# Low words of the weights and first key copies on GpSimd instead of ScalarE, with all steps in another order of issue

## The chip, the core and the metric

The kernel runs on one core of one Trainium2 chip. The metric is device time in microseconds (us). Five engines work side by side, each through its own instructions in order: TensorE (matmuls, PE in the profile, its weight loads PEld), VectorE (DVE), ScalarE (ACT), GpSimd (POOL) and SyncE (SP), which here issues every transfer (DMA). An instruction waits on semaphores for what it needs, and while it waits everything behind it on the same engine waits too.

## What is computed

A gated delta-rule attention over 4 batches of 8 heads, 768 tokens of 48 features, and behind it an MLP mixer over tokens and channels. Cut to what matters:

```python
k_n = k / (np.linalg.norm(k, axis=-1, keepdims=True) + 1e-06)
for t in range(S):
    y[:, :, t] = q_t @ state                     # per batch and head
    state = state + beta_t * outer(k_t, v_t - k_t @ state)
x = y as (B, S, H*D)
h = np.maximum(x.transpose(0, 2, 1) @ w_tok1, 0.0) @ w_tok2
u = x + h.transpose(0, 2, 1)
return u + np.maximum(u @ w_ch1, 0.0) @ w_ch2    # float32
```

q, k, v and beta come as float32. The four weight matrices come as float64 (768x256, 256x768, 384x1536, 1536x384), and the kernel turns them into float32 on the chip.

## The kernel before

**Units and steps.** The sequence is cut into 24 units of 128 tokens of one batch (all 8 heads of it). The recurrence over tokens is done in 36 steps: r0 to r23 take 64 tokens of batches 0 and 1, r24 to r35 take 64 tokens of batches 2 and 3 together. Before a unit can be walked, its triangular 64x64 blocks have to be inverted; units are inverted in rounds (i0 takes units 0 to 3, i1 takes 4 and 5, later ones up to four).

**Jobs.** Every part of the work is a Python generator whose `yield`s cut it into steps. For a unit u: `k` loads keys and queries (`load_kq`, L406), `v` loads and scales values (L449), `p` makes norms, masks and turned copies (`prep`, L528), `c` and `d` make the products of keys with keys and queries (`grams`, L504), `t` hands the diagonal blocks to the inversion (`to_parts`, L668), `h`, `f` and `j` put the inverse together. `i` is the inversion of a round (L717), `r` a recurrence step (`recur`, L903; `recur_pair`, L983), `m` the mixer of batches 0 and 1 (L1586), and `T`, `A`, `F`, `B` that of batches 2 and 3. `w0` to `w33` each turn one piece of a weight matrix into float32 (`round_weights`, L271). `x`, `z` and `Y` issue matmuls on zeros.

**The order.** One long string (L1775 to L1845) lists 2610 steps; a loop takes them one after the other and calls `next` on the job named. So the string alone sets the order of instructions on every engine and of transfers on the sync queue. Semaphores and buffers are put in by the framework; assertions in the jobs say what must have been issued before.

**A weight piece** (128 rows, 384 or 256 columns) has four steps. Step 0 loads it as 64-bit words into one of three landing buffers `d64` (L280); a fourth piece can only be loaded when the first one's buffer has been read for the last time. Step 1 is two ScalarE instructions, one on the high words of the float64s (L286) and one on the low words (L287), both in place and with a stride of two words. Step 2 shifts the high words on VectorE (L289). Step 3 adds the two on GpSimd as integers into the resident weight (L293), and frees the landing buffer.

**Keys of the first units.** Units 0 to 3 have their keys stacked from the padded copy that is on the chip already, by four copies of 64 partitions each (L435, on ScalarE); half of these copies go from one half of the partitions to the other. Later units load the stacked form from memory (`stacked`, L440). Step 0 of `p` (L539) squares the stacked keys on ScalarE.

**Into the first inversion.** `t0` to `t3` each have a ScalarE copy (L674), a VectorE copy (L677) and a GpSimd copy (L679), and i0 begins with a VectorE transpose of what the four have written (L731). The inversion then runs on VectorE in pairs of small instructions (L739, L744).

**A recurrence step** is a chain: matmuls (L920), a VectorE subtraction (L927), matmuls (L940, L944), a ScalarE copy (L950), matmuls (L958, L959), a VectorE update of the state (L967) and two ScalarE copies of the output (L972).

Of the kernel before, what the change touches and what calls it, by code (L numbers as in the profile page):

```python
# [23 lines left out]
def kernel(  # L24
# [102 lines left out]
    for par in range(2):  # L127
        for n0, n1, first in ((0, (B - 1) * NP, par), ((B - 1) * NP, B * NP, 1 - par)):
            nc.gpsimd.tensor_copy(
                out=pick[:, par, n0:n1],  # L130
                in_=ident[: B * H, 2 * n0 + first : 2 * n1 : 2],
# [139 lines left out]
    def round_weights(dst, src, name):  # L271

        n = dst.shape[-1]
        d64 = loads.tile([128, WP], mybir.dt.int64, name="d64", bufs=3)[:, 0:n]
        nc.sync.dma_start(out=d64, in_=src)  # L280
# [5 lines left out]
        nc.scalar.activation(a, a, ACTF.Prelu, scale=2.0**-112, alpha=2.0**32)  # L286
        nc.scalar.activation(lo, lo, ACTF.Copy, scale=2.0**-29)  # L287
        yield
        nc.vector.tensor_scalar(  # L289
            out=f, in0=hi, scalar1=3, scalar2=None, op0=ALU.logical_shift_left,  # L290
        )
        yield
        nc.gpsimd.tensor_tensor(out=dst.bitcast(U32), in0=f, in1=lo, op=ALU.add)  # L293
# [112 lines left out]
    def load_kq(u):  # L406
# [25 lines left out]
        heads = kpad[slot(u)].rearrange("t (p par) d -> t p par d", par=2)  # L432
        for cc in range(2 if u < RU else 0):
            for par in range(2):
                nc.scalar.copy(kst[PAR[par ^ cc], :, cc], heads[PAR[cc], :, par, 0:D])  # L435
# [1346 lines left out]
    h0 h1 h0 w8*2 h1 Y i0 f0 Y p4 f1 h2*2 p5*3 f0*2 w6 h0*5 k6*5 p6 z f2*2 k8*3 p5
    w6 p5 p3 p5 j0*3 f1*2 h1*5 j0*2 w8*2 w17 f2 h2*3 v0 t4*2 w17 r0*5 p6 h2*2 c5*2
    v1 w11*2 j1 p5 k7*2 c5 k7 c5 r0 c5 r0*2 w14*2 v1 w11*2 k7*2 p7 d5*5 r1*5 w14*2
    p6*2 t5 j1 t5*2 r1*2 j1 j2 p7 h3*2 r1*3 p6*3 i1*2 r2*5 k8*2 f3*2 w9 k9*3 j1*2
    v2*2 i1*3 j2*2 r2*2 f3 i1*2 p6*3 w16 v2 w16*3 r2*2 h3 r2 i1 d6 r3*5 i1*2 w9*3
    v2 d6 h3 v2 w0 h3*2 r3 h3 d6*2 w0 d6 j3 c6*5 r3*4 w0 j2 w0 p8*2 j2 r4 p8 r4*4
# [8 lines left out]
    i2*2 r10*4 w12 i2 k12 i2*2 m0 w32 k11 k12 w32 r10*2 m0 p11 k12*4 w19 p11 r10  # L1796
    c10 r10 c10 r10 w33 d10*2 q2 Y r11*4 v7 r11*3 w19 c10 q1 w30 c10 r11 k12*2
    i2*3 r11 v6*4 i2*5 m0*3 i2*5 q5 i2 m0 p11*4 c10 p11 m0 p11*2 m0*2 k12*2 w12
    m0*3 v6 f6*3 w12 d11 c11*2 d11*2 c11 w33 c11 d11*2 j6 p12 w12 m0 w33 w30*3
    p12*2 f7*3 j6*2 m0 c11 j7 f6 f8 w27*2 f8 j7 f8 w15 f7 m0 w29 w33 w29 j7 r12*4  # L1800
    w31 j8 p11 t10*3 r12 Y r12 f9 j8 f9 w21 p12 r12 f8 r13*2 w15*2 r12 w15 r13*3
    w31*3 Y r13*2 w33 j8 w21 m0 r13 q4 p12*4 r13*2 m0*2 r14 c12 f9 j9 r14*2 w21
    t10 w20*2 v7 r14*2 c12*2 w33 c12 r14 v8 c12*2 r14*2 w25*2 j9 r14 r15 v8 w21
    r14 r15 w25 r15*3 w25 k13*4 w20 k13*4 p13 k13*2 w20 v8*3 m0*2 p13 w25 p13 m0
    r15 p13 r15 p13 w27 w25 k13*2 j9 m0*4 p13 f9 w23 t12*3 p13 t12 w25 r15*3 c13*6
    w23 k14*7 r16*5 m0 p13 m0*3 w23*4 k14 r16*2 t11 t13*2 j9*2 t11*3 w33 p14 r16*2
    p14*2 w31 m0*3 w31 m0 w31 m0 w23 r17*2 r16 t13 r17 t13 r17*2 p14*2 m0*2 p14 i3
    k14*4 i3*3 k15 v9*2 m0*3 v10 i3*5 k15 i3 r17 k15*2 p14 k15*3 m0 v10*2 i3 k15*2
    m0*2 k15*2 i3*4 r17*4 k15 i3*2 p14 m0*2 i3*6 m0*4 r18 i3 r18*2 v9*3 r18*2 i3*8
    m0*10 v10*2 m0 r18 c14*4 r18*2 m0*2 f10 c14 f10*2 f12*2 p15*3 m0*4 r18 r19 r18  # L1810
    r19*3 j10 f10 j10*2 f12 p15 f11*4 f12 r19 c14 r19 v11 p15*3 k16*7 j11 m0*2
    r19*4 j11 j12 r20*3 k16*2 r20 m0 r20 k16*3 v11 m0 j11 r20*2 v11*2 p15 c15*2
    p10 r20*2 c15 r20 c15*3 f13*3 p16 r21*5 m0 r21*2 p16*4 k17*7 p16 j12*2 p16 k17
    r21*3 m0*3 r22 c16 r22*3 k17*4 v11 r22 c16*4 r22*2 m0 r22 t14 p17 f13 c16 t14
    j13*2 t14 r22 r23 t15*2 t16 r23*2 r22 r23 m0*3 r23 t15*2 r23 p17*5 t16 p17 j13
    t16*2 m0*3 t14 c17*5 r23*2 c17 t17*2 m0*8 p17 t17*2 i4*3 v12 m0 k18 v15*2 i4
    m0 i4 m0 i4*3 m0 i4 k18*2 j13 p16 m0*2 j13 i4*4 m0 v12*3 k18*4 v12 k18 r24*2
    r23 v13*5 m0 k18*4 v15*2 i4*2 m0*2 p18 i4 p18 r24*3 m0 r24 i4 m0 p18*2 r25*4
    p18 k19*8 i4 m1 r25 i4 m1*4 i4 m1 v14 i4*2 v14 i4*8 r24*3 r25*2 m1 v14 i4*2
    v14*2 p18*2 r25 m1*2 p19 m1*5 k19*4 p19 f14*2 r25*5 c18*5 f14 c18 p18 r26*3  # L1820
    p19*2 j14 p19*3 r26*2 f15*4 f14 m1*2 j14 m1 j14 j15*3 s*2 f17*2 m1 f17 m1
    f16*3 p19 f16 k20*8 j16*3 j17 m1 r26*3 p20 m1*2 p20 r26*2 c19*2 r26 c19 v15
# [60 lines left out]
```

## Time and profile before

| | us |
|---|---|
| median of 3 runs | 625.72 |
| the runs | 620.05, 625.72, 627.02 |
| span of the profiled execution | 619.7 |
| TensorE busy in it | 590.3 (95%) |
| VectorE busy | 469.1 (76%) |
| ScalarE busy | 256.9 (41%) |
| GpSimd busy | 109.9 (18%) |
| moved by DMA | 55.52 MB, mean 90 GB/s |

The profiled execution's own time is its span, 619.7 us; it lies 0.4 us under the fastest run and 6.0 under the median. A row of a group reads: line, engine, operation, output<-inputs, shapes, count, then busy time in us and mean ns of one, then the idle time of the engine just ahead of these instructions and what ended it. A row of the timeline reads: start in us, duration in us, engine, line, operation, and in brackets the idle time ahead and what ended it. Ends of matmuls are modelled, so a busy TensorE isn't TensorE at its peak.

### The profile page before, as it was taken

Reading aid. Unit: us, or ns where it says so; the run is one execution under the profiler, and the core shown is the slowest. Engines: PE = TensorE matmul, PEld = TensorE weight load, DVE = VectorE, ACT = ScalarE, POOL = GpSimd, SP = SyncE. Lnnn points to the kernel's source line nnn. Section 1 sums busy time; section 2 is a strip of 40 time slices with the busy share of each in tenths; the row PEclk is TensorE's granted clock in tenths of the full one; section 3 lists DMA queues with packets and bytes.
Section 4 is the critical chain, followed back from the end, with each engine's and each line's share of the span. In section 5 each row is a group of like instructions: output and inputs, shape, how many; then the busy total and the mean of one; then the engine's idle time right before and its main releaser. Section 6 shows DMA issues by size and latency. Waiting matters only on the chain.

```text
span 619.7 us, 20909 instructions
## 1 busy us (share of the span) xinstructions
PE 590.3 (95%) x8733; PEld 515.9 (83%) x8733; DVE 469.1 (76%) x1160; ACT 256.9 (41%) x682; POOL 109.9 (18%) x150
## 2 busy tenths in 40 slices
PE   8588997999999999999999999999999999999998
PEld 5467875667898988877889888897699999999997
DVE  5987875986889855697566996866888898685874
ACT  8758796448521344223551215415352331414200
POOL 2348264225311122003020120010000000000000
PEclk9878797999999999999999999999999999999999
DMA  9667567667653254454445443135102012020001
GB/s 219 136 135 169 138 142 185 129 155 179 126 114 72 67 116 83 95 113 99 92 87 126 83 95 83 32 66 140 32 2 39 1 21 47 12 52 13 14 26 51
DMA packets 154605, 55.52 MB, mean 90 GB/s; under 512 B 129648, under 2 KB 148976, under 8 KB 154512
## 3 DMA queue, kind: packets, MB, share of 16 engines
q1 hardware_dynamic: 154512, 54.20, 39.1%
q8 instruction: 68, 1.11, 0.8%
q14 instruction: 25, 0.20, 0.1%
HBM read 41.19 MB, written 11.21 MB: 85 GB/s over the span
## 4 chain that ended last, share of the span: by engine, by line
PE 74%; DVE 9%; DMA 4%; ACT 4%; issue 2%; SPq 1%; POOL 1%; DVEq 0%; POOLq 0%; ACTq 0%
PE p_c L1668 13%; PE p_r L1498 13%; PE p_o L1689 10%; PE p_a L1570 7%; PE p_b L1570 6%; PE p_g L511 3%; DMA d<-in_moe_w_ch_dram 3%; PE p_h L1608 3%; DVE sub L739 2%; PE p L1593 2%; DVE x L744 2%; PE p_k L920 2%; PE p L1223 1%; PE p_h L1238 1%; PE p_y L1034 1%
## 5 line engine op out<-in xcount | busy, mean ns | idle before, releaser
L1668 PE MATMUL p_c<-u_t,wc 128*128 128x256 f32 x432 | 101.6, 386 | 0.5 <-issue 0.5
L1668 PEld LDWEIGHTS p_c<-u_t,wc 128*128 128x128 f32 x432 | 79.6, 190 | 11.9 <-issue 1.1
L1689 PE MATMUL p_o<-wc,r 128*128 128x192 f32 x360 | 64.6, 331 | 0.7 <-DVE xb L1628 0.7
L739 DVE TENSOR_TENSOR sub<-x 128x84 f32<-128x84 f32 (+24 forms) x178 | 58.4, 328 | 7.4 <-DMA x<-n_dram 2.8
L744 DVE TENSOR_TENSOR x<-x,sub 128x84 f32<-128x84 f32 (+24 forms) x178 | 58.2, 327 | 6.1
L1689 PEld LDWEIGHTS p_o<-wc,r 128*128 128x128 f32 x360 | 58.4, 190 | 2.3 <-DVE xb L1628 1.3
L1677 ACT ACTIVATE r<-p_c 128x512 f32<-128x512 f32 x36 | 21.4, 596 | 51.2 <-PE p_c L1668 46.1
L511 PE MATMUL p_g<-kq 48*64 48x128 f32 (+1 forms) x704 | 34.9, 283 | 4.0 <-ACT kq L587 3.3
L517 DVE TENSOR_TENSOR gm<-p_g,mb 128x512 f32<-128x512 f32 x44 | 28.9, 683 | 8.1 <-PE p_g L511 7.5
L484 POOL TENSOR_TENSOR v_st<-v_st,nrm 128x384 f32<-128x384 f32 x12 | 10.3, 856 | 131.9 <-DMA v_st<-in_v_dram 104.4
L574 POOL TENSOR_TENSOR mb<-mask_c,cs 128x512 f32<-128x512 f32 x20 | 21.2, 1062 | 67.8 <-DVE cs L552 36.9
L511 PEld LDWEIGHTS p_g<-kq 48*64 48x64 f32 (+1 forms) x704 | 26.5, 137 | 7.6 <-ACT kq L587 4.3
L293 POOL TENSOR_TENSOR wc<-w_f,d 128x384 uint32<-128x384 uint32 x24 | 24.6, 1029 | 42.8 <-ACT d L287 14.1
L1511 DVE TENSOR_TENSOR kq<-kq,p_r 128x384 f32<-128x384 f32 x40 | 21.0, 551 | 10.7 <-PE p_r L1498 8.8
L1498 PE MATMUL p_r<-t_d,wc 128*128 128x192 f32 x160 | 28.8, 326 | 0.0
L1511 DVE TENSOR_TENSOR gm<-gm,p_r 128x384 f32<-128x384 f32 x40 | 21.1, 551 | 8.1 <-PE p_r L1498 5.8
L400 DVE STREAM_TRANSPOSE kq<-pads 128x512 f32<-128x512 f32 x24 | 25.5, 1108 | 2.0 <-PE p_w L1038 1.6
L1498 PEld LDWEIGHTS p_r<-t_d,wc 128*128 128x128 f32 x160 | 26.5, 190 | 0.0
L1689 PE MATMUL p_o<-wc,s 128*128 128x192 f32 x144 | 25.7, 330 | 0.6 <-DVE xb L1628 0.6
L1498 PE MATMUL p_r<-pads,wc 128*128 128x192 f32 x128 | 25.4, 326 | 0.0
L1628 DVE TENSOR_TENSOR xb<-xb,p_o 128x192 f32<-128x192 f32 x42 | 14.6, 348 | 13.0 <-PE p_o L1689 12.6
L1689 PEld LDWEIGHTS p_o<-wc,s 128*128 128x128 f32 x144 | 23.3, 190 | 1.2 <-DVE xb L1628 0.9
(315 smaller groups left out, 1387.1 us busy)
## 6 DMA issues: line engine op xcount, KB each, us to landing
d<-in_moe_w_ch_dram SPq DMA_DIRECT2D x24, 384.0 KB, 4.2
v_st<-in_v_dram SPq DMA_DIRECT2D x96, 48.0 KB, 2.9
out_dram<-xb SPq DMA_DIRECT2D x23, 192.0 KB, 2.1
kst<-in_k_dram SPq DMA_DIRECT2D x64, 48.0 KB, 2.8
n_dram<-gm SPq DMA_DIRECT2D x72, 32.0 KB, 2.3
pads<-in_k_dram SPq DMA_DIRECT2D x24, 96.0 KB, 2.9
...
```

What stands on the lines that cost most here:

```text
L293: nc.gpsimd.tensor_tensor(out=dst.bitcast(U32), in0=f, in1=lo, op=ALU.add)
L400: nc.vector.transpose(kq_of[p // 2][:, i, :, p % 2].rearrange("f p (s g) -> f p g s", g=G), rows_of[i].rearrange("s p (g d) -> s p g d", g ...
L511: nc.tensor.matmul(p_g[PAR[i ^ cc ^ swap(u)], p], kqt[f, p, cc, 0], kqt[f, p, cc])
L517: nc.vector.tensor_tensor(out=blocks(gm_of(u))[:, :, cc, D:GW].rearrange("s p (two n) -> s p two n", two=2), in0=p_g, in1=made[u][:, :, cc ...
L739: nc.vector.tensor_tensor(out=tmp, in0=y[:, :, 0:s, s : s + 1].to_broadcast([n, k, s, w]), in1=y[:, :, s : s + 1, s + 1 : m].to_broadcast( ...
L744: nc.vector.tensor_tensor(out=y[:, :, 0:s, s + 1 : m], in0=y[:, :, 0:s, s + 1 : m], in1=tmp, op=ALU.add,)
L1498: nc.tensor.matmul(p[:, i], pieces[q // width][:, at : at + 128], f[f"u{n}"], start=first and i == 0, stop=True, skip_group_check=True,)
L1511: nc.vector.tensor_tensor(out=o, in0=o, in1=p, op=op_of(sign))
L1570: nc.tensor.matmul(p, a[:, i], w[:, i // 2, i % 2], start=first and i == 0, stop=True, skip_group_check=True,)
L1668: nc.tensor.matmul(p_c[:, k], piece_of(wc1, cb, f * 128)[:, f * 128 : (f + 1) * 128], u_t[:, cb], start=(cb == 0), stop=(cb == NCB - 1),)
L1677: nc.scalar.activation(r2[:, m], p_c, ACTF.Relu)
L1689: nc.tensor.matmul(p, a[:, m], wc2[:, m, j], start=(start and i == 0), stop=(i == NM - 1), skip_group_check=True,)
```

## The change

Two instructions change their engine, and the order string is another one. The jobs, the transfers, the buffers and the number of steps of each job stay as they are (2610 steps, the same count for every job, the `x`, `z` and `Y` among them).

```diff
         nc.scalar.activation(a, a, ACTF.Prelu, scale=2.0**-112, alpha=2.0**32)
-        nc.scalar.activation(lo, lo, ACTF.Copy, scale=2.0**-29)
+        nc.gpsimd.tensor_scalar(out=lo, in0=lo, scalar1=2.0**-29, scalar2=None, op0=ALU.mult)
...
-                nc.scalar.copy(kst[PAR[par ^ cc], :, cc], heads[PAR[cc], :, par, 0:D])
+                nc.gpsimd.tensor_copy(out=kst[PAR[par ^ cc], :, cc], in_=heads[PAR[cc], :, par, 0:D])
```

The first is issued 34 times (28 of 128x384 words, 6 of 128x256), the second 16 times (64 partitions, 4 runs of 48 words). The string, in its first lines before and after:

```diff
-    w10 x*4 z w10*2 z w1*4 k1*3 z k1*3 z b p1 z p1 k0*6 p0*2 b*2 p1 w2 p0*5 p1*2
-    w10 p0*2 z w3 w2 c0*3 p0 w3*2 d0*2 w3 c0 p1 c0 d0*3 k2*3 v1 p1*2 w18 k2*2 p1*2
-    c1*2 d1 k2 p2*2 c1 t0 d1 c1*2 d1*3 t0 p2*8 c2*2 w2 d2 c2*3 Y d2 w2 k3*6 p3
-    d2*2 p3 d2 t1*3 x p3*7 c3 k4*5 k7 w13 w18*2 d3*2 v1*2 v0*2 c3*3 v0 c3 d3*3 t0
...
+    w10 x*2 w10*2 w1 x*2 w1 k1 Y k1*4 z k1 b w1 k0*2 w1 k0*4 z*4 p1*2 w3 b*2
+    p0*10 k2*2 k3 k2 k3 w2 p1*2 w10 w3 k3 p1 z c0 k2 d0 c0*2 k2*2 p2 w3 p2 c0
+    d0*2 c0 p2 k3 d0*2 p1*5 k3 w18 x w3 t0 c1 k3 c1*3 d1 c1 d1 p2 d1*3 t0 k4 k5
+    k4*3 w2 p2*5 x*2 c2*3 p2 c2*2 d2*2 w13 p3*2 t1 w13 w18 w2 w18 w2 d2 p3 d2*2
+    p3*2 t0 t1 k4 p3*3 k5 p3 d3*3 k5 d3 w18 d3 c3*5 t2 t1 p4*2 k5*2 t3 t2*2 k6 t3
```

And around the recurrence steps r8 to r11 (the whole string is reordered in this manner, each job's own steps in their sequence):

```diff
-    w27*2 w7*2 d9*4 c9*2 f5 c9*3 t7*2 t8 r7*2 t7*2 j4*2 v4 p10*2 h5 r8*3 w29 t8*3
-    w29 w27*2 r8*2 w29*2 q3 w29 j4*2 r8 w22*4 t9*3 r8*3 p9 r9 p10 r9*3 t9 v5 h5*3
-    j5 i2 r9 w4*2 r8 h5 i2*5 w4 i2 w19*2 k10 w32 p10*2 w32 v7 k12 m0*2 k11 k12 q0
-    v5*3 p10*2 r9*2 j5*2 k11*3 i2*2 r9 w4 i2 j5 i2*3 p10 v5 r9*2 d10*3 r10 v7*2 j5
...
+    w7 w22 d9*3 f5 d9 f5 p9 c9*5 t9*2 r7 t9*2 v4 r8*3 w29 j4*2 h5 k11 i2 w27 j4
+    w27 j4 h5 r8*2 w27 Y*2 w29 r8*2 p10*3 r8*2 w29 r9*2 w4 r9 w22 r9*2 r8 h5*2 r9
+    w22 j5 p10*2 v6 r9 i2 w19 h5 i2 p10*2 r9 i2*2 q2 r9 i2 d10 w4*2 i2 p10 m0
+    i2*2 k11 v5*2 w22 j5 d10 j5 i2*2 r10*4 i2*2 v5*3 w32 w19*2 k11 r9 i2 k11 p11
+    k11 r10 j5 i2 w4 w19 m0 i2 m0 p11 j5 r10 w12 w30 m0 k12*3 r10*2 i2*2 d10 p11
```

The weight pieces come in nearly the same sequence in both (w10, w1, then w2 and w3 in turn, w18, w13, w17, and so on).

More of the change, by code (lines that the diff above doesn't have):

```diff
@@ L1782 @@
[L1782 to L1787, printed above, removed]
@@ L1795 @@
-    v5*3 p10*2 r9*2 j5*2 k11*3 i2*2 r9 w4 i2 j5 i2*3 p10 v5 r9*2 d10*3 r10 v7*2 j5
[L1796 to L1822, printed above, removed]
@@ new lines @@
+    p4*2 t3 i0*5 w13 i0*3 k7 i0*3 p5 i0*2 p4*2 w13 v0 k5 k6 v0 p4 w17 i0*2 k4
+    p4*2 d4*2 c4 d4*2 v1 c4*2 w8 v0*2 w6 w8 p4 w6 i0 c4*2 w17 d4 Y*2 k8 z k6 z p5
+    z*2 v1*2 w6 k6 v1 h0*2 t4 k6 p5 h1*2 v1 i0 w6 f0 f1 f0 k6 f1 p5*2 h2 p5 f0 h0
+    x h0 p3 h0*2 f1 h0 w14 p5 k7 p5 h2 w8*2 f2*3 j0*2 p6 j0 p5 t4 h1*4 k7 j1 k7
+    w11 h1 j0*2 v0 w14 k7 h2*4 c5 h2 w14*2 w0 r0 w17 r0*3 c5*3 d5*2 p6 r0*2 p6
+    d5*2 t4 c5 r0 p5 r0 p7 r1*3 p6 r1*2 w11 j1 d5 k8 t5 r1 p7 r1 h3*2 r1 p6 j1
+    w11 p6 t5 j2 f3*2 r1 r2*2 w17 r2*2 j1*2 v2 t5 i1 r2 j2 p6 r1 v2 j2 r2 i1*6 f3
@@ new lines @@
+    r7*2 d8 h4*2 w27 d8 t8*4 h4*2 r7*2 h4 t7 p10 p9*3 p8 p9 r7 j4 r7 p9 d9 q3 f5
+    w7 w22 d9*3 f5 d9 f5 p9 c9*5 t9*2 r7 t9*2 v4 r8*3 w29 j4*2 h5 k11 i2 w27 j4
[3 more added lines that the diff above has]
+    k11 r10 j5 i2 w4 w19 m0 i2 m0 p11 j5 r10 w12 w30 m0 k12*3 r10*2 i2*2 d10 p11
+    c10*2 r10 w32 k12*3 w32 d10 c10*2 r11 k12 r11*2 k12*2 r11 d10 r11 Y r10 r11
@@ new lines @@
+    q0 v7 r11 i2 w12 r11*2 p11 i2 w12 v6 i2 m0 i2 w32 k12 i2 k12*2 w12 i2 q5 p12
+    m0 v7 v6 w33 w15 i2*6 v6 p11 m0 i2*2 p11 v7*2 m0 c10 p11*3 m0*3 f6 m0 f6*2
+    w33 m0*2 f7*2 d11 f7 f6 f9 c11 p11 f8 f9*2 f7 c11*4 f8*2 w15*3 w30*2 j6 d11*3
+    w30 w33 d11 t11 m0 j6*2 t11 f9 w33 m0 f8 j7 w33 j7 w33 m0 j7 w25 p12 v6 r12*4
+    p12*2 r12*2 j8*2 r12 r13*3 r12 w27*2 v7 s j9 j8 r13 w21 m0 r13 w31 q4 p12 k13
+    w25 k13*7 p12 r13 p12 m0 r13*2 p12 c12*2 r13 k13 w31*3 r14*2 w20 q1 r14*2 r13
+    c12*2 r14 v8 c12*2 r14 w25 r14 w27 w21 k13*2 t12 r14*2 j9 r14 r15 w21*2 r15*4
@@ new lines @@
+    m0*7 f11*3 m0*3 p15 f12 r18 c14*4 f12 r18*3 f11 r18 m0 k15 m0 j10 m0*3 p15
+    r19*4 v10 p15 r19 j10*2 p15 r19*2 c14 p15 j11 m0 f12 r19*3 p15 j11*2 r20*4
+    p15 r20 m0 c15 k16*5 r20*2 m0 k16*4 r20 k16*3 r20*2 c15*4 v11 r21*5 v11*2 c15
+    t15 v11 j12 m0 p16 r21*2 p16 f13*2 p16*5 t15*2 k17 j12 k17*3 r21*3 j12 t15
+    m0*3 r22*2 v11 k17*3 r22*2 k17*5 c16*2 r22 c16*2 r22*2 v12*2 m0 c16*2 j13 v12
+    r22 v12 r22 j13 r23 j13 r22 r23*4 m0 j13 p17 t16 p17*2 j13 r23*2 m0*3 v12
+    p17*4 m0 c17*5 k18*3 r23 c17 r24*2 m0*2 r23 r24*2 t16 r24 t14*2 t16 t14*2
@@ new lines @@
+    t17*2 m0 t17 r24 m0*4 t17 t16 v13 i4 k18 p16 k18*2 i4*2 v13 m0 v13 k18 i4
+    m0*2 v14*4 i4*3 m0*3 p17 m0 i4*4 v13*2 m0*2 i4 k18 m0 k18 m0*2 i4*2 m0*2
+    p18*2 i4*2 m0 i4*2 m1 r25*5 k18*2 p18*3 k19*5 p18 k19 r24 k19*2 r24 m1*5 i4*4
+    r25*2 i4*7 k18 m1*2 v15*3 r24 i4 v15 i4*2 p19 p18 m1*2 k19*4 m1*2 p19 f14*2
+    r25 f17 m1*2 f14 c18 r25*3 f14 f15 p19 f15*2 c18*2 r25*2 f16 p19 v15 f15 r25
+    c18*2 f16 j14 c18 r26*4 p19 f16 k20*4 p19 m1 v14 t18 j14 p18 k20*3 j14 k20 m1
+    j15*3 j16 f17 t18 f17*2 m1 p19 m1 r26 j16 k20 j16 m1*3 k20 r26 f16 k20 v16
@@ L1846 @@
+    A2 A1*4 A2 B0*2 A2 A1*4 W A1*7 F0 A1*16 F0*2 A1*6 F0*2 A1*13 F0*2 A1*4 B0 A1
+    A2 W F0*2 B0*2 A1 B0*5 A2*2 B0*3 A2*2 F0 F1*2 A2*3 F1 B0*10 F1 B0 A2*13 F1*2
+    B1 A2*7 B0 A2*25 A3 A2*11 B1 A2 A3*2 A2*5 F1*3 B1*2 A2*3 A3*2 F1 B1*7 F1 F2
+    B1*4 A3 A2 F2*2 B1 A3 B1*3 A3 F1*3 A3*3 F1 B1*6 A3*13 B1*3 A3*12 F2 B1 A3
+    F2*3 A3*6 B2 A3*4 F2*2 A3*30 B1 F2 B2*2 F2 B2*6 F3*2 F2*2 B2*2 F2*2 B2*6 F3
+    B2*3 F3*3 B2*3 F3 B2*2 F3*5 B2*5 F3*3 B3*30
     """
```

64 lines of the change are left out of this document (35 added, 29 removed).

## The prediction

> **What bounds the kernel now.** I read the table by stretches first: busy microseconds of TensorE, its weight loads, VectorE, ScalarE and GpSimd, then the granted TensorE clock and the DMA share.
>
> ```profile
> core 0: us, PE busy (x) PEld busy (x) DVE busy (x) ACT busy (x) POOL busy (x), PEclk, DMA share, GB/s
> 0.00:27.00 27.00, 20.14 (x246) 14.70 (x246) 18.41 (x55) 22.52 (x59) 8.18 (x23) 1.00 0.74 169
> 41.30:53.10 11.80, 10.54 (x298) 9.17 (x295) 9.63 (x15) 11.09 (x32) 7.46 (x10) 1.00 0.55 119
> 96.00:125.00 29.00, 24.16 (x496) 17.73 (x491) 22.37 (x63) 14.29 (x40) 9.47 (x11) 0.82 0.69 160
> 58.57:68.81 10.24, 10.24 (x244) 9.24 (x242) 7.96 (x22) 7.35 (x20) 3.84 (x5) 0.50 0.58 130
> 99.53:109.77 10.24, 7.42 (x74) 5.06 (x66) 5.97 (x21) 4.64 (x14) 3.87 (x6) 0.50 0.77 210
> 0.00:160.00 160.00, 137.17 (x2872) 106.77 (x2873) 123.35 (x320) 110.05 (x293) 69.11 (x95) 0.90 0.68 157
> 160.00:441.00 281.00, 277.53 (x4801) 236.82 (x4799) 208.19 (x535) 97.18 (x285) 40.80 (x56) 1.00 0.42 93
> 441.00:619.70 178.70, 175.56 (x1065) 172.29 (x1063) 137.59 (x307) 49.64 (x105) 0.00 (x0) 1.00 0.11 24
> ```
>
> From 160 us on TensorE is busy 98% and more, so what is left there is a fixed amount of matrix work; both orders issue the same matmuls, and no edited instruction runs there but one (the last low word, at 168.5 us). The end moves only by what moves the first 160 us. There no engine is full: VectorE 77%, ScalarE 69%, GpSimd 43%, DMA 0.68. That is a chain that passes from engine to engine, and the edits touch two of them. ScalarE is the tightest in two places (22.52 of 27 us, then 11.09 of 11.8). Two stretches of 10.24 us ran at half the clock.
>
> Then I read which waits TensorE has on ScalarE (table of waits from 10 to 125 us: total, times, longest), and ScalarE's timeline around 101 to 112 us:
>
> ```profile
> PE p_s L958 <- ACT rw_t L950: 3.5, 5, 2.0
> PE p_g L511 <- ACT kq L587: 3.3, 4, 1.4
> ```
>
> ```profile
> 101.02 0.55 ACT L286 ACTIVATE d<-d 128x384 f32<-128x384 f32 x1 [1.93 <-DMA d<-in_moe_w_ch_dram]
> 101.46 0.56 ACT L287 ACTIVATE d<-d 128x384 uint32<-128x384 uint32 x1
> 102.05 0.32 ACT L950 COPY rw_t<-p_w 128x192 f32<-128x192 f32 x1
> ...
> 106.94 0.44 ACT L286 ACTIVATE d<-d 128x256 f32<-128x256 f32 x1 [3.88 <-DMA d<-in_moe_w_tok_dram]
> ...
> 111.67 0.56 ACT L286 ACTIVATE d<-d 128x384 f32<-128x384 f32 x1 [1.42 <-DMA d<-in_moe_w_ch_dram]
> ```
>
> ScalarE stands still 1.93 + 3.88 + 1.42 = 7.2 us for weight pieces, and what stands behind each piece is the recurrence: the copy of step r8 (L950, 102.05) goes only after piece w22, and r8's outputs after w4.
>
> **The change part by part.** What moves from ScalarE to GpSimd, with the rows nearest to its new price (count: least/median/greatest ns):
>
> ```profile
> L287 ACT ACTIVATE d<-d x34: 420/545/579, 4.4 to 168.5; 128x384 uint32<-128x384 uint32 x28, 128x256 uint32<-128x256 uint32 x6
> ```
>
> ```profile
> L435 ACT COPY kst<-pads x8: 340/349/352, 5.5 to 8.8; 64x192 f32<-64x192 f32 x8
> L435 ACT COPY lent<-lent x8: 348/349/358, 13.5 to 19.1; 64x192 f32<-64x192 f32 x8
> ```
>
> ```profile
> L293 POOL TENSOR_TENSOR wc<-w_f,d 128x384 uint32<-128x384 uint32 x24 | 24.6, 1029 | 42.8 <-ACT d L287 14.1 <-DVE w_f L289 13.3 <-issue 7.6
> ...
> L293 POOL TENSOR_TENSOR w<-w_f,d 128x256 uint32<-128x256 uint32 x6 | 4.4, 738 | 18.1 <-DVE w_f L289 17.8 <-issue 0.3
> ...
> L679 POOL COPY r<-gm 32x256 f32<-32x256 f32 x4 | 3.0, 739 | 3.3 <-ACT r L674 2.5 <-ACT nrm L547 0.7
> ```
>
> ```profile
> L129 POOL COPY pick<-ident 32x12 f32<-32x12 f32 (+1 forms) x4 | 0.6, 184 | 0.1
> L124 POOL COPY mask_c<-mask_f 64x64 f32<-64x64 f32 x2 | 0.5, 232 | 0.1
> ```
>
> ScalarE loses 34 x 0.545 less the shorter forms, 18.1 us, and 16 x 0.35 = 5.6 us: 23.7 of its 110. GpSimd has no one-input operation of 384 strided words in the trace. From below: the two small copies differ by 48 ns over 52 words, 0.92 ns a word, so 384 words take 0.53 us and 256 take 0.41. From above: the add on the very same words, with two inputs, at 1.03 and 0.74. I take the middle, 0.75 and 0.55, since the stride is the add's and the single input is the copy's. That is 28 x 0.75 + 6 x 0.55 = 24.3 us (17.3 to 33.3). A key copy has 192 words in runs of 48: 0.35 by the slope, 0.55 by L679, whose words lie far apart; I take 0.35, so 5.6 us (to 8.9). GpSimd gets +30 us (23 to 42), nearly all within 160 us: 69 becomes about 99, 62% of the stretch. The first key copies start nearly where they did: w10 and w1 have landed by 4.4 us, their low words end at 4.4 + 0.75 + 0.55 = 5.7, and the copies began at 5.5.
>
> *E, the price that GpSimd time has on VectorE.* Around 36 us, and the first and the last of such places before 160 us:
>
> ```profile
> 36.16 0.20 DVE L739 TENSOR_TENSOR sub<-x 128x28 f32<-128x28 f32 x1
> 36.38 1.01 POOL L293 TENSOR_TENSOR wc<-w_f,d 128x384 uint32<-128x384 uint32 x1 [7.59 <-issue]
> 36.39 1.06 DVE L744 TENSOR_TENSOR x<-x,sub 128x28 f32<-128x28 f32 x1
> ```
>
> ```profile
> 21.73 0.55 DVE L677 COPY r<-wc 32x256 f32<-32x256 f32 x1
> ```
>
> ```profile
> 159.20 1.18 DVE L1648 TENSOR_TENSOR s<-s,r 128x384 f32<-128x384 f32 x1
> ```
>
> L744 takes 1.06 us where its twin L739 took 0.20: it lasts until GpSimd's add is done. I counted 23 such VectorE rows from 21.73 to 159.20 us, each beside a GpSimd instruction and over 0.1 us longer than the shortest of its shape; together they lose 12 us to 69 us of GpSimd, 0.17 us for each. So +30 us cost VectorE 5.1 (3.9 to 7.2). VectorE is busy 77% there, so I put +4 on the path (0 to +7). A held instruction never gets faster, so there is no gain at this end. [...]
>
> *A, up to the first inversion (i0).* Today its transpose starts when the fourth corner copy is done on GpSimd:
>
> ```profile
> 25.84 0.85 POOL L679 COPY r<-gm 32x256 f32<-32x256 f32 x1 [0.65 <-ACT nrm L547]
> ```
>
> ```profile
> 26.73 1.95 DVE L731 STREAM_TRANSPOSE x<-r 128x1024 f32<-128x1024 f32 x1
> ```
>
> ```profile
> 12.22 2.00 SPq L420 DMA_DIRECT2D pads<-in_k_dram  x1
> 14.33 3.18 SPq L444 DMA_DIRECT2D kst<-in_k_dram  x4
> ```
>
> ```profile
> DMA to landing us min/median/max: 3.2/4.2/7.3
> ```
>
> In the new order GpSimd has, ahead of the four corner copies, the low words of w2, w13 and w18, and the low word is a new wait: it stands still until its piece has landed. Queued behind w13's are w18's low word, w2's add, the corner copies t0 to t3 with w18's add among them, and so i0. The sync queue issues w13 as its 20th transfer, behind unit 4's pad and stacked keys (to 17.5 us today) and one more pad of unit 5 (some 0.4 us): about 18.0; landed 4.2 later, 22.2; behind it 2 x 0.75 + 0.74 + 1.03 + 4 x 0.74 = 6.2 us: i0 at 28.4 against 26.7, **+1.7 us**. With 7.3 us to landing and the upper price, +5; if w13 is early, ScalarE's lighter load (8 copies and 4 low words fewer ahead of i0) lets VectorE start it up to 2 us sooner.
>
> *B, from i0's end to the first recurrence copy.* ScalarE is full (11.09 of 11.8), but I counted what each order issues there from step 15 of i0 to r0's copy: 34 instructions of 14.0 us before, 35 of 14.0 after, since w14's high word and two join copies come in. **0** (-1 to +2).
>
> *C, the stalls at r8 and r9.* In the new order w22 stands behind r8's copy, w4 behind r9's copy and w32 behind r10's. The 7.2 us of standing still leave the recurrence; GpSimd now stands still for the same pieces, and v5's scaling, which r10 and r11 need, is queued behind w4's low word and w22's add. **-5** (-7.2 to 0).
>
> *D, ScalarE lighter elsewhere.* The two waits of TensorE make 6.8 us; ScalarE has about a fifth less to do; **-2** (-6.8 to 0).
>
> *G, the clock.* The half-clock stretch at 99.53 has TensorE busy 7.42 us, so at most 3.7 lost; it falls on the stalls of C. The one at 58.57 is full: 5.1 lost. **-1** (-3.7 to +5).
>
> *F, the rest.* All else that moves by some places, transfers and recurrences after 160 us among it, is hidden behind TensorE's work (277.53 of 281 us); without that cover its idle 3.5 us could double. **0** (-2 to +3).
>
> Sum: +4 + 1.7 + 0 - 5 - 2 - 1 + 0 = -2.3 us, so the span goes from 619.7 to 617.4. The profiled execution stands at the fast end of the runs (620.05, 625.72, 627.02); the shift on their median gives **623 us**.
>
> **The rivals.** *Faster, 615.* GpSimd's new work fits into its idle time: low price (E +1), A 0, C -7.2, D -4, G -1: -11, 615 us. For it: ScalarE at 83% and 94% where the chain is young; 91 us of GpSimd idle before 160. Against: E is seen 23 times. *Slower, 633.* GpSimd becomes the bound of the early chain: low words at 1.03 us and a late w13 give A +5, E +7, and v5 behind w4 takes C down to -2, D -2: +8, 633 us. It decides once w13 lands after about 24 us, so that A is over 3.5, and a low word costs 0.9 or more. For it: the one queue behind one transfer; against: GpSimd is idle 57%. *The relief does nothing, 626.* The weight stream (three landing buffers, a transfer share of 0.68) and the recurrence set the pace, ScalarE's time was never on the path, C's standing still only changes engine, E is hidden: 0.
>
> **How the numbers follow.** Faster case 0.36, slower case 0.20, the sum 0.30, nothing 0.14. One per cent is 6.3 us, about what a measurement of this kernel can tell from no change. So faster by over 1% 0.36, within 0.44, slower by over 1% 0.20. The likeliest case alone runs from 619.5 to 628. The bounds of A, C, E and G reach further to both sides: 612 to 633.
>
> **What would show it.** Today the Relu behind the first token matmuls marks the point from which TensorE is fed:
>
> ```profile
> 125.95 0.49 ACT L1603 ACTIVATE r<-p 128x384 f32<-128x384 f32 x1 [1.52 <-PE p L1593]
> ```
>
> Right: a low word on GpSimd near 0.75 us; ScalarE busy about 86 us and GpSimd about 99 before 160; i0's transpose near 28 us; no ScalarE wait of 2 to 4 us for a weight piece ahead of r8's and r9's copies; some 28 to 32 held VectorE rows; that Relu at about 123.5. Wrong: i0 after 31 us (A, the slower case), a low word at 1 us, the Relu at 118 or before (the faster case), or a rest after 160 us that changes by more than 3 us (F).

## The result, and the profile after

| | before | after |
|---|---|---|
| median (4 runs each, same chip) | 624.89 us | 662.03 us |
| the runs | 620.05 to 627.02 | 659.25 to 666.10 |
| ratio | 1 | 1.0618 [1.0556, 1.0679] |
| span of the profiled execution | 619.7 | 659.2 |

The change makes the kernel 6% slower. The forecast was 623 us, the range 612 to 633, the slower rival 633. The ratios compare fast runs alone; for e5 to e8 below, three slow runs of the kernel before (625.6, 627.9 and 629.8 us) are left out of the ratio but not of its median of 624.4 us.

The same table by stretches as before, of the profile after (core, busy us of TensorE, its loads, VectorE, ScalarE, GpSimd, granted clock, DMA share; the cuts are later, since the stages are):

```profile
0.00:160.00 160.00, 130.78 (x2460) 102.87 (x2460) 116.11 (x292) 81.63 (x216) 103.51 (x132) 0.84 0.59 140
160.00:480.00 320.00, 302.47 (x5209) 256.38 (x5210) 227.57 (x564) 105.98 (x312) 53.37 (x69) 0.97 0.41 90
480.00:659.20 179.20, 175.98 (x1066) 172.48 (x1064) 134.31 (x305) 49.29 (x105) 0.00 (x0) 1.00 0.11 24
```

In the middle stretch TensorE was busy 277.53 of 281 us; now it is idle 17.5 of 320, and the clock is 0.97 where it was 1.00. The last stretch has hardly changed. The busy line and the chain that ended last (before, then after) say the same: TensorE's share of the chain was 74% and is 44%, and VectorE, with the small instructions of the inversion (L739, L744: 2% each before, 6% each now), the transfers and the sync queue have more of it.

```profile
PE 74%; DVE 9%; DMA 4%; ACT 4%; issue 2%; SPq 1%; POOL 1%; DVEq 0%; POOLq 0%; ACTq 0%
```

```profile
PE 609.2 (92%) x8733; PEld 531.7 (81%) x8733; DVE 478.0 (73%) x1160; ACT 236.9 (36%) x632; POOL 156.9 (24%) x200
...
PE 44%; DVE 19%; DMA 9%; SPq 7%; issue 4%; POOL 2%; ACT 2%; DVEq 0%; POOLq 0%; ACTq 0%
```

The rows that the prediction named. Low words and key copies on GpSimd (count, shapes, busy us, mean ns):

```profile
L287 POOL TENSOR_SCALAR d<-d 128x384 uint32<-128x384 uint32 x28 | 35.4, 1266 | 11.8 <-DMA d<-in_moe_w_ch_dram 8.2 <-DMA d<-in_moe_w_tok_dram 1.7
L287 POOL TENSOR_SCALAR d<-d 128x256 uint32<-128x256 uint32 x6 | 5.4, 898 | 1.1 <-DMA d<-in_moe_w_tok_dram 0.5 <-ACT gm L795 0.3
L435 POOL COPY lent<-lent 64x192 f32<-64x192 f32 x8 | 3.4, 431 | 0.7 <-DMA lent<-in_k_dram 0.3
L435 POOL COPY kst<-pads 64x192 f32<-64x192 f32 x8 | 2.7, 341 | 0.3
```

The first inversion's transpose, the first recurrence copy and the Relu that marks the feeding of TensorE (first start 30.1, 62.1 and 141.8 us; before 26.7, 52.8 and 125.95):

```profile
L731 DVE STREAM_TRANSPOSE x<-r x2: 1902/1934/1965, 30.1 to 68.7; 128x1024 f32<-128x1024 f32 x2
```

```profile
62.12 0.32 ACT L950 COPY rw_t<-p_w 128x192 f32<-128x192 f32 x1 [0.15 <-PE p_w L944]
```

```profile
L1603 ACT ACTIVATE r<-p x4: 490/490/491, 141.8 to 307.2; 128x384 f32<-128x384 f32 x4
```

So 15.9 us are lost up to the Relu: 3.4 up to i0's transpose, 6.0 from there to r0's copy, 6.5 from there to the Relu. The first step of the last part (A0) starts at 480.0 instead of 440.8: another 23.3 us are lost in the stretch that the prediction held for covered. From there to the end both traces run alike.

**The account that closes.** For each trace I took from the start to the last matmul TensorE's idle time, and for the stretches at clock 0.50 half of its busy time in them. What remains is nearly the same number in these kernels:

| kernel | median | TensorE busy | idle | lost to half clock | busy less that |
|---|---|---|---|---|---|
| before | 624.9 | 590.3 | 26.5 | 12.4 | 577.9 |
| after | 662.0 | 609.2 | 47.0 | 31.0 | 578.2 |
| e1, order alone | 661.9 | 608.5 | 47.0 | 28.9 | 579.6 |
| e2, low words alone | 630.8 | 593.3 | 31.8 | 14.2 | 579.1 |
| e3, key copies alone | 630.1 | 596.0 | 27.6 | 17.3 | 578.7 |
| e5, new head | 644.3 | 600.4 | 36.8 | 20.4 | 580.0 |
| e6, new tail | 646.6 | 597.0 | 39.5 | 17.6 | 579.4 |
| e18, e6 with the old sync order | 663.1 | 605.7 | 48.8 | 23.5 | 582.2 |

In the other traces it lies between 573.5 (e10) and 582.6 us, but for e11 and e12, which issue more matmuls. The work is the same 578 us; the change adds 20.5 us of idle TensorE and 18.6 us of half clock, 39.1 of the 39.4 by which the last matmul is later. Most of the half clock is no separate accident but follows idle time. Here is one place of the after trace, cut at its own steps of 3.41 us:

```profile
343.90:347.32 3.42, 3.42 (x53) 2.94 (x44) 1.22 (x3) 0.00 (x0) 0.32 (x1) 1.00 0.36 71
347.32:350.73 3.41, 1.53 (x39) 1.20 (x37) 1.46 (x4) 1.38 (x5) 0.00 (x0) 1.00 0.69 139
350.73:354.14 3.41, 3.10 (x89) 2.73 (x79) 3.36 (x6) 2.62 (x9) 1.20 (x2) 0.50 0.46 77
354.14:357.56 3.42, 3.42 (x37) 3.09 (x30) 1.42 (x3) 0.43 (x1) 0.00 (x0) 0.50 0.30 62
357.56:360.97 3.41, 3.41 (x98) 2.94 (x98) 1.06 (x3) 2.16 (x6) 0.83 (x1) 1.00 0.53 96
```

TensorE is busy 1.53 of 3.41 us (one wait of 1.9), and in the next step the clock is 0.50; after one full step it is back, in other stretches only after several. All 160 half-clock stretches of the 20 traces (this document's kernels) start on such a grid, with a phase of its own in each run. Of the steps at full clock in which TensorE was busy under half, 77 of 79 were followed by half clock; of those busy 0.5 to 0.6, about half; of some 2600 steps busy over 0.95, none. By these numbers, as an estimate, idle time of over 1.7 us in one step costs about as much once again behind it, and more where the half clock lasts longer.

### The profile page after: what moved, and what is told of

Read it like the earlier page. It is cut to its first block, busy times and chain, and to the rows that moved or that the text cites. A ratio compares the mean times of both kernels' runs of the same rounds, so it can differ in the third digit from the quotient of the medians.

```text
span 659.2 us, 20895 instructions
## 1 busy us (share of the span) xinstructions
PE 609.2 (92%) x8733; PEld 531.7 (81%) x8733; DVE 478.0 (73%) x1160; ACT 236.9 (36%) x632; POOL 156.9 (24%) x200
## 4 chain that ended last, share of the span: by engine, by line
PE 44%; DVE 19%; DMA 9%; SPq 7%; issue 4%; POOL 2%; ACT 2%; DVEq 0%; POOLq 0%; ACTq 0%
PE p_r L1498 11%; PE p_a L1570 6%; DVE x L744 6%; DVE sub L739 6%; PE p_b L1570 6%; PE p_o L1689 4%; PE p_c L1668 2%; SPq L686 2%; DMA x<-n_dram 2%; SPq L711 2%; PE p L1593 2%; DMA w_dram<-x 2%; DMA kst<-in_k_dram 1%; SPq L444 1%; PE p_g L511 1%
## 5 line engine op out<-in xcount | busy, mean ns | idle before, releaser
L1668 PE MATMUL p_c<-u_t,wc 128*128 128x256 f32 x432 | 103.0, 393 | 0.0
L1668 PEld LDWEIGHTS p_c<-u_t,wc 128*128 128x128 f32 x432 | 82.1, 195 | 12.1 <-issue 0.3
L739 DVE TENSOR_TENSOR sub<-x 128x84 f32<-128x84 f32 (+24 forms) x178 | 61.7, 347 | 15.7 <-DMA x<-n_dram 11.2
L1689 PE MATMUL p_o<-wc,r 128*128 128x192 f32 x360 | 67.7, 337 | 3.9 <-DVE xb L1628 3.9
L744 DVE TENSOR_TENSOR x<-x,sub 128x84 f32<-128x84 f32 (+24 forms) x178 | 65.8, 370 | 6.1
L1689 PEld LDWEIGHTS p_o<-wc,r 128*128 128x128 f32 x360 | 59.0, 192 | 7.1 <-DVE xb L1628 5.4
L287 POOL TENSOR_SCALAR d<-d 128x384 uint32<-128x384 uint32 (+1 forms) x34 | 40.8, 1201 | 12.9 <-DMA d<-in_moe_w_ch_dram 8.2
L511 PE MATMUL p_g<-kq 48*64 48x128 f32 (+1 forms) x704 | 38.3, 303 | 5.3 <-DVE kq L400 2.8
L511 PEld LDWEIGHTS p_g<-kq 48*64 48x64 f32 (+1 forms) x704 | 28.7, 149 | 8.3 <-ACT kq L587 3.7
L293 POOL TENSOR_TENSOR wc<-w_f,d 128x384 uint32<-128x384 uint32 x24 | 24.2, 1012 | 24.1 <-DVE w_f L289 23.3
L1511 DVE TENSOR_TENSOR gm<-gm,p_r 128x384 f32<-128x384 f32 x40 | 20.8, 547 | 7.7 <-PE p_r L1498 5.0
L1689 PE MATMUL p_o<-wc,s 128*128 128x192 f32 x144 | 26.0, 331 | 0.3 <-DVE xb L1628 0.2
L539 ACT ACTIVATE ksq<-kst 128x384 f32<-128x384 f32 x18 | 9.4, 523 | 46.1 <-DMA kst<-in_k_dram 43.3
```

The source lines that it names most:

```text
L287: nc.gpsimd.tensor_scalar(out=lo, in0=lo, scalar1=2.0**-29, scalar2=None, op0=ALU.mult)
L511: nc.tensor.matmul(p_g[PAR[i ^ cc ^ swap(u)], p], kqt[f, p, cc, 0], kqt[f, p, cc])
L739: nc.vector.tensor_tensor(out=tmp, in0=y[:, :, 0:s, s : s + 1].to_broadcast([n, k, s, w]), in1=y[:, :, s : s + 1, s + 1 : m].to_broadcast( ...
L744: nc.vector.tensor_tensor(out=y[:, :, 0:s, s + 1 : m], in0=y[:, :, 0:s, s + 1 : m], in1=tmp, op=ALU.add,)
L1511: nc.vector.tensor_tensor(out=o, in0=o, in1=p, op=op_of(sign))
L1668: nc.tensor.matmul(p_c[:, k], piece_of(wc1, cb, f * 128)[:, f * 128 : (f + 1) * 128], u_t[:, cb], start=(cb == 0), stop=(cb == NCB - 1),)
```

## The experiments

Each was timed beside the kernel before on its chip (medians there 623.0 to 624.4 us). "Head" is the order up to the first step of inversion round i3 (181 us before), "tail" what follows. Where nothing else is said, both moved instructions are back on ScalarE.

**e1 to e4: the parts apart.** Theory 1 lays the loss on GpSimd's price of 1.27 us for a low word, theory 2 on the order, theory 3 on the two together. e1 has the new order alone, e2 and e3 one moved instruction each in the old order, e4 the new order with the key copies.

```diff
-        nc.scalar.activation(lo, lo, ACTF.Copy, scale=2.0**-29)
+        nc.gpsimd.tensor_scalar(out=lo, in0=lo, scalar1=2.0**-29, scalar2=None, op0=ALU.mult)
```

> The new order with both operations left on ScalarE. Theory 1 (the price of the low word on GpSimd, 1.27 us where 0.75 was taken, delays the early chain and holds VectorE; the order is harmless): 615 to 628 us, weight pieces done by about 172 us. Theory 2 (the order itself costs, in its later part too, where no edited instruction runs): about 640 to 645 us, that is the 20 us by which the delay still grows after 189 us in the changed kernel. Theory 3 (order and price only hurt together, since the new order counts on short low words): 615 to 628 us here and under 640 for the low words alone.

> The old order with the low words on GpSimd, keys on ScalarE. Theory 1: 645 to 660 us, most of the 37 us. Theory 2: about 640 us, the 16 us that were lost up to the first token Relu and nothing more. Theory 3: under 640, less than half of the loss.

> The old order with the key copies alone on GpSimd. All theories: within 5 us of before (620 to 628), since a copy takes 0.34 us on GpSimd and 0.35 on ScalarE; slower by over 5 would mean that the crossing copies or their queue matter.

> The new order with the key copies on GpSimd and the low words on ScalarE. Theory 1: as the order alone or some us faster, 612 to 626 us. Theory 2: about 640 us. Theory 3: as theory 1.

Measured: e1 661.87 us, 1.0612 [1.0557, 1.0668]; e2 630.82, 1.0127 [1.0083, 1.0171]; e3 630.14, 1.0109 [1.0067, 1.0150]; e4 662.21, 1.0617 [1.055, 1.0684]. The order alone makes the whole loss. In the new order the engine moves cost nothing at the end (661.9, 662.2, 662.0), though i0 starts 3.5 us and the Relu 2.6 us earlier in the after trace than in e1's. In the old order each costs 7 to 8 us, a little over 1% and clear of noise. Both of these losses lie ahead of the Relu, which comes at 132.9 us in e2 and 133.2 in e3 (125.95 before). In e3, which all theories had within 5 us of before, a copy takes the expected 0.34 us, but in the trace the copies stand behind GpSimd's adds for weight pieces, ScalarE's squares (L539) wait 9.3 us for them, and i0 starts at 31.5 us instead of 26.7. Theories 1 and 3 fall; theory 2 had the cause, but too small a size for the order and too large a one for the low words (640 forecast in e2).

**e5, e6: which half.** e5 is the new head with the rest old, e6 the old head with the rest new. The order string at the seam, old against e6:

```diff
-    p14*2 m0*2 p14 i3 k14*4 i3*3 k15 v9*2 m0*3 v10 i3*5 k15 i3
+    k14*4 r17*2 v10*2 r17*2 i3 p14*2 i3*3 r18*2 i3*4 v10 k15 r18*2 k15
```

> The new order up to the first step of inversion round i3 (about 177 us before), then every step that is left in the old order; both engine moves undone. The new order alone cost 38.5 us, of which the start of i3 showed about 17 to 20. Theory 2a (both halves cost, each by itself): 640 us. Theory 2b (the late start does all the harm and what follows inherits it): 655 to 662. Theory 2c (the second half costs everything once TensorE is full): 623 to 630.

> The old order up to the first step of i3, then the steps that are left in the new order; both engine moves undone. Theory 2a: 645 us (22 us grow after i3). Theory 2b: 620 to 628. Theory 2c: 655 to 662. The prediction's step F, that all order after 160 us is hidden, asks for 621 to 626.

Measured: e5 644.34 us, 1.0409 [1.0315, 1.0503]; e6 646.63, 1.0440 [1.0349, 1.0531]. Theory 2a holds: 20 and 22 us by the medians (25 and 27 by the ratios). In the traces the span grows by 20.4 and 19.8 us, together close to the 38.7 of e1's. In e5's trace r25 to A0 start 19.3 to 20.7 us late throughout; e6 is nearly on time at i3 (+1.8) and loses 5 us by i4, 7 by i5 and 6 from there to A0. The tail costs by itself, entered on time: that is the prediction's step F, refuted.

**e7, e8: which steps of the tail.** Steps that feed the recurrence (k, v, p, t, i) were put back to their old places in the new tail (e7), or alone to their new places in the old one (e8), as far as pairs of steps that stand alike in both orders allow. Around i4, e6 against e7:

```diff
-    t17 t16 v13 i4 k18 p16 k18*2 i4*2 v13 m0 v13
+    t17*2 v12 j13*2 k18 m0 t17 m0*4 t17 i4*3 k18*2 p16 m0 i4 m0*2 p17
```

> As e6, but in the new second half the steps that feed the recurrence (loads and preparation k, v, p, and the inversion rounds t, i) are put back to their old places, as far as the two orders leave room; recurrence, mixer and the joins stay new. Theory Q (the order of the feed and of the sync queue costs the second half): 621 to 629. Theory R (the order of recurrence, mixer and joins among themselves costs it): 638 to 645.

> The old order, in which only the feed (k, v, p, t, i after the start of i3) stands at its new places. Theory Q: 638 to 645 us. Theory R: 621 to 629.

Measured: e7 656.64 us, 1.0596 [1.0494, 1.0699]; e8 640.99, 1.0340 [1.0257, 1.0423]. The feed at new places costs 17 us (21 by the ratio), as theory Q had it; putting it back costs 10 more than leaving it, which neither Q nor R foresaw. So the feed's new order costs by itself, and yet the old one, among new neighbours, is worse than either the old tail or the new.

**e9, e10: two queues' waits.** In e6 the sync queue stands for the mixer's output stores (L1631), in e5 for landing buffers (L280):

```profile
SPq L1631 <- DVE xb L1628: 17.2, 5, 8.7
SPq L1631 <- DVE sub L739: 12.7, 3, 5.9
```

```profile
SPq L280 <- POOL wc L293: 20.6, 5, 7.4
SPq L280 <- POOL w L293: 7.8, 4, 6.4
```

(us in total, times, longest; the kernel before: 7.5 and 15.4 us for these pairs of rows.) e9 issues four of six pairs of stores later, e10 puts all steps of the weight pieces back to their old places in e5.

```diff
-            store(c)
...
-            store(c + 1)
+            if c == NCH - 2:
+                store(c)
+                store(c + 1)
+            else:
+                unsent.extend([lambda c=c: store(c), lambda c=c: store(c + 1)])
```

> The order of e6 (old up to i3, new behind it), in which four of the mixer's six pairs of output tiles are stored six or more mixer steps later than their last sum; the last pair of each batch is stored where it was. In e6 the sync queue stands 6.4, 5.6, 4.3 and 3.3 us for such stores (8.7 more for a last pair, which stays) with the loads of later units behind them; before, 2.2 us at most. Theory S (these stores hold up the loads, and so inversion and recurrence): 632 to 640 us, and the waits on L1631 gone but for one. Theory D (the second half loses by many small places, no one of them decides): 643 to 649, as e6.

> The order of e5 (new up to i3, old behind it), in which all steps of the weight pieces stand at their old places. In the new order a piece is loaded only 1 to 25 steps after the step that frees its landing buffer (old: 26 to 80), and the sync queue stands 34 us for landing buffers (before 9.9), 7.5 us twice ahead of the first recurrence step. Theory H (that standing makes the first half late): 626 to 634 us. Theory D (many small places): 640 to 648, as e5.

Measured: e9 649.02 us, 1.0421 [1.0378, 1.0464], where e6 had 646.6 (1.0440); e10 653.17, 1.0495 [1.0453, 1.0538], where e5 had 644.3. The stores' waits did shrink, from 29.9 us to one row:

```profile
SPq L1633 <- DVE xb L1630: 9.7, 3, 8.7
```

and the landing buffers' from 28.4 to 18.2, and nothing was gained: e9 is as slow as e6, and e10's A0 starts 10.6 us later than e5's. Theories S and H fall as forecasts, but neither edit took the waiting out of the queue. It stands at other lines instead: in all it waits 98.0 us from 160 to 460 us in e6 and 92.3 in e9 (107.6 in the kernel before), and 60.5 us up to 200 us in e5 and 67.3 in e10 (45.7 before). So a long wait of this queue doesn't show by itself what it costs; what a queue with less waiting would be worth wasn't tested.

**e11, e12: filling the gaps.** Matmuls on zeros ahead of each instruction that TensorE had stood for, in the old and in the new order; one of eleven places:

```diff
-    p4 i0*2 p4*2
+    p4 i0*2 x*17 p4*2
```

> The kernel before, with 45 more matmuls of 128 columns on zeros (9.6 us of TensorE) put into its eleven idle gaps of over 0.5 us ahead of 145 us, 70% of each gap. The computation is the same. Theory C (an idle share of TensorE in a stretch of 3.4 us brings half the clock in the next; that costs 12.4 us before): 611 to 620 us, with fewer half-clock stretches. Theory C' (the clock does not follow from these gaps, or the zeros delay the real matmuls as much as they save): 622 to 632.

> The new order with both engine moves undone (e1, 661.9 us), with 77 such matmuls (16.4 us) in its fourteen gaps of over 0.5 us ahead of 145 us. There the half clock costs 22.6 us, before 12.4. Theory C: 640 to 652 us. Theory C': 660 to 668.

Measured: e11 627.42 us, 1.0062 [1.0028, 1.0096]; e12 660.13, 1.0607 [1.0565, 1.0649]. The half clock costs less in e12 (20.0 us for 28.9) and hardly less in e11 (11.2 for 12.4), while what isn't idle or half clock grew by 11.6 and 20.8 us: the zeros took the time that they saved. No gain came of it; on whether a filled gap keeps the clock it is inconclusive, since gaps moved elsewhere.

**e13, e15, e16: one wait.** In e6's trace VectorE stands for the keys of unit 21, and the product that TensorE needs is queued behind:

```profile
327.85 0.55 DVE L542 TENSOR_REDUCE ksum<-ksq 128x8 f32<-128x384 f32 x1 [4.67 <-ACT ksq L539]
328.32 0.68 DVE L517 TENSOR_TENSOR gm<-p_g,mb 128x512 f32<-128x512 f32 x1
```

```profile
329.06 0.64 PE L884 MATMUL p_x<-gm,zst 32*32 32x32 f32 x28 [3.10 <-DVE gm L517]
```

e13 (on e6) and e15 (on e1) put that product first; e16 makes the old order like e6 there.

```diff
-    c20 t18 c20 p20 p21 r27 c20 v17*2 r28*4 v17 r28 c20*2 p21*2 c20
+    c20 t18 c20 p20 r27 c20 v17*2 r28*4 v17 r28 c20*3 p21*3
```

> The order of e6 with one change: the first three steps of preparation p21 (square on ScalarE, sum and reciprocal on VectorE) stand behind the last step of c20 instead of ahead of it (17, 2 and 1 places). In e6 VectorE stands 4.67 us and ScalarE 6.98 us for unit 21's keys, with c20's last product behind them; TensorE stands 3.1 us for that product ahead of j17 and then runs 6.8 us at half clock (3.4 us lost). Theory W (single waits with an operand of TensorE behind them): 6.5 us less than e6, 638 to 643. Theory D (spread; another wait takes this one's place): 645 to 650.

> The whole new order (both engine moves undone, e1: 661.9 us) with the same change at p21. There TensorE stands 2.7 us at j17 and loses 4.6 us to the half clock behind it. Theory W: 653 to 657 us. Theory D: 660 to 664.

> The old order with one change the other way round: the last two steps of c20 stand behind the loads of unit 21 and the first two steps of p21, so that VectorE waits for unit 21's keys with c20's last product behind that wait. Theory W: a new wait of 3 to 7 us and a half-clock stretch: 627 to 634 us. Theory D, or TensorE has other work at hand there: 622 to 626.

Measured: e13 642.76 us, 1.0336 [1.0277, 1.0395]; e15 663.42, 1.0664 [1.0609, 1.072]; e16 622.26, 0.9974 [0.9941, 1.0008]. e13 is 3.9 us under e6 by the medians, at the edge of theory W's range, but the intervals overlap, and in the traces A0 starts at 460.4 us in e13 and 460.3 in e6; e15 gains nothing. The stall has gone from its place, and 2.4 us stand at the next instruction behind the same keys, this time by way of ScalarE:

```profile
327.33 0.52 ACT L539 ACTIVATE ksq<-kst 128x384 f32<-128x384 f32 x1 [5.61 <-DMA kst<-in_k_dram]
...
329.04 0.66 ACT L1072 ACTIVATE xb<-p_y 64x192 f32<-64x192 f32 x2
```

```profile
329.75 0.25 PE L1038 MATMUL p_w<-rw_t,gm 64*64 64x48 f32 x1 [2.41 <-ACT xb L1072]
```

The square of the keys starts at 327.3 us in both. As a cure theory W isn't borne out: the instruction behind the late operand was moved in front, and the next one that needs it stands there instead. In e16 VectorE does stand 2.8 us for unit 21's keys (0.1 before), with c20's last product behind them, but TensorE stands only 0.3 us for that product: it has other work at hand, and the wait costs nothing.

**e14: the head, cut once more.** New up to r0, then old.

```diff
-    k7 h2*4 c5 h2 w14*2 w0 r0 w17 r0*3 c5*3 d5*2 p6 r0*2 p6
+    h2 w14*2 w0 k8*3 w17 t4 w17 r0*5 p6 c5 w11 p5 c5*2 r0 c5 r0*2
```

> The new order up to the first recurrence step r0 (some 60 us), then every step that is left in the old order; both engine moves undone. In e5 r0 started 12.0 us late and the end came 20 us late. If the loss up to r0 stays as it is: 633 to 637 us. If the old order makes it up: 623 to 628.

Measured: 634.37 us, 1.0208 [1.0143, 1.0272], as the first case said (by the interval 9 to 17 us more than before). The loss up to r0 (11.0 us in its trace, and 11.0 at A0) stays to the end; nothing later makes it up. Some 9 of the head's 20 us come after r0.

**e17, e18: one engine's own order back.** Why the keys of unit 21 are late can be followed in e6's trace: GpSimd stands 16.66 us for values (v16), p20's products are behind it, and the load of the keys waits for these. e17 gives GpSimd its old sequence in e6, e18 the sync queue its own.

```diff
-    c19 v16 p20*2 r27 j17*2 k21*2 t19 m1 s r27 k21 r27 k21 c20 t18 c20 p20
+    c19 p20*2 r27 j17*2 k21*2 m1 r27 k21 r27 k21 c20*2 p20 v16 t19 s t18
```

> The order of e6, in which only GpSimd's own sequence is as in the old order (31 pairs of its steps change places, v16's scaling and p20's products among them); all else keeps its new place as far as that leaves room. Theory G (GpSimd standing for values, with the release of key buffers behind it, is the root at i5): the stall of 3.1 us at j17 and its half-clock stretch go, 638 to 641 us, or down to 632 if it is the root at i4 and i6 as well. Theory D (spread): 643 to 650.

> The order of e6, in which only the sync queue's own sequence of transfers is as in the old order (1117 pairs change places). Theory Q (the order of transfers makes the second half late): 625 to 635 us. Theory G or D: 640 to 655.

Measured: e17 655.69 us, 1.0516 [1.0461, 1.057]; e18 663.14, 1.0630 [1.0589, 1.0671]; e6 had 646.6. No range holds them: e17 lies above both theories', e18 above all. Each cures what it was made for in part. In e17 the stall at j17 shrinks from 3.1 to 1.0 us, while ScalarE's waits for keys stay (41.8 us); in e18 ScalarE's waits for keys fall from 38.1 us to this, near the 4.7 of before:

```profile
ACT ksq L539 <- DMA kst<-in_k_dram: 10.6, 5, 3.4
```

But TensorE now stands elsewhere. In e17:

```profile
354.28 3.48 PE L1689 MATMUL p_o<-wc,r 128*128 128x192 f32 x18 [3.62 <-DVE xb L1628]
...
363.11 0.34 PE L1038 MATMUL p_w<-rw_t,gm 64*64 64x48 f32 x1 [4.88 <-DVE rw_t L1018]
```

and in e18:

```profile
351.75 0.34 PE L1038 MATMUL p_w<-rw_t,gm 64*64 64x48 f32 x1 [5.02 <-DVE rw_t L1018]
```

Theories G and Q fall too. Restoring one queue out of five costs 9 and 16.5 us by the medians; e17's interval overlaps e6's, but none of its runs is under 653.1 us and none of e6's over 648.9. What is left is theory D, in a form that no run confirms alone: in the tail, from 160 us to A0, TensorE has ten to sixteen waits of 0.5 us or more in each trace with a new tail (three before, the longest 0.6 us), the longest of 2.2 us in the after trace, 3.1 in e6's and 7.8 in e7's. That the fit of the five sequences to one another makes or removes them is the reading that agrees with e7, e17 and e18; it isn't shown by itself. No run here is faster than the kernel before, clear of noise.

## Why the prediction was wrong, step by step

**F failed, "all else that moves by some places ... after 160 us ... is hidden behind TensorE's work (277.53 of 281 us)", 0 (-2 to +3).** The tail's order costs some 20 us alone (e6); in the after trace the way from the Relu to A0 takes 23.3 us more than before: 13.7 of idle TensorE, 8.4 of half clock, the rest between. The row was read rightly and used wrongly. That TensorE is full tells that the old order has every operand there in time; it isn't a cover that a new order inherits. That both orders issue the same matmuls was right, and it is the 578 us. The other terms' sizes alone don't explain the miss: even all upper bounds of the sum together make +22 us, or 648, where 662 was measured.

**G failed in sign, -1 (-3.7 to +5).** Up to the Relu the half clock costs 22.7 us instead of 12.4, so +10.3. It was treated as something to be shifted; it mostly follows stalls, so that a stall has to be priced nearly twice (20.5 us of idle time came with 18.6 of half clock in the whole).

**B failed, 0 (-1 to +2).** From i0's start to r0's copy it takes 32.0 us, before 26.0. The number of ScalarE instructions was not what set this stage. Two of the 6.0 us lie ahead of the first join (L777): i0's steps on VectorE take 13.0 us from its first transpose to its second, before 11.1, with six of its rows held to over 0.4 us beside GpSimd's work, before one. TensorE has nothing else to do there from 41.1 us on and stands 5.1 us at the join. The other four lie behind it, where TensorE runs at half clock from 43.5 to 64.0 (half clock that is also counted in G). The first join before and after, and the stretch:

```profile
PE p_z L777 <- DVE gm L517: 1.1, 1, 1.1
```

```profile
PE p_z L777 <- DVE gm L517: 5.1, 1, 5.1
```

```profile
48.90:62.10 13.20, 12.96 (x243) 11.86 (x241) 6.79 (x14) 10.33 (x30) 7.61 (x9) 0.50 0.32 78
```

**The low word was mis-sized**, 1.27 and 0.90 us for 0.75 and 0.55, above the upper bounds of 1.03 and 0.74 that the add with two inputs gave. GpSimd got 34.4 us more up to 160 us (103.51 busy, 69.11 before) and 47.0 in all (156.9 for 109.9), where 30 was forecast and 42 the bound. It did no harm at the end in this order (e1 against after), so the error did not decide. In the old order the low words cost 7.8 us (e2); how much of that is the price beyond 0.75 us isn't shown.

**E was about right for VectorE's time.** 39 VectorE rows are held up to 160 us instead of 24 (by one count on both traces; 28 to 32 forecast), 3.9 us more, where 5.1 was forecast; what of it is on the path is not shown apart. **A was right in mechanism**: i0 at 30.1 us, 28.4 forecast, 31.7 the bound. GpSimd stands still for w13, which lands at 22.3 us (22.2 forecast), and most of what A has too little is the price of the two low words there:

```profile
22.32 2.72 POOL L287 TENSOR_SCALAR d<-d 128x384 uint32<-128x384 uint32 x2 [4.25 <-DMA d<-in_moe_w_ch_dram]
```

In e1, with the key copies on ScalarE, i0 starts at 33.6 us, in e4 at 30.1; the 3.5 us that this move brings forward are lost again by the Relu in e4 (144.4 us, e1 144.5).

**C and D came to nothing.** ScalarE is lighter (81.63 us to 160, 86 forecast), and no wait for a piece stands ahead of r8 and r9. But TensorE then stands 3.9 us at r10 for VectorE. The matmuls of r10 ahead of its subtraction (L927) are done and v5's values scaled by 123.7 us; the subtraction starts only at 131.0, since VectorE works without a pause on i2 until then. The new order puts nine steps of i2 between r9's update of the state and r10's subtraction, the old order two:

```profile
129.97 1.09 DVE L744 TENSOR_TENSOR x<-x,sub 128x234 f32<-128x234 f32 x1
130.99 0.34 DVE L927 TENSOR_TENSOR rw_t<-p_k,v_st 128x192 f32<-128x192 f32 x1
```

e1 has 4.6 us there without GpSimd's low words. So it is the place of i2's steps in the order, not the low word ahead of v5 that the prediction named. That the moves relieve nothing was the third rival, at 0.14; for the moves alone in this order it came true at the end (e1 against after), but its 626 us for the whole change did not.

**The rivals** all shared F. The slower one found its mechanism in the engine moves: of its two conditions the dear low word was met, the late w13 was not. None let the order itself cost. Still open is which neighbourhoods of the new order would have to change together to win the 38 us back; the seven cures that were tried (e7, e9, e10, e13, e15, e17, e18) gave no answer.
